# Row sums of two head pairs in one pass of four 32-column tiles, reciprocals spread through DRAM, q and k prep grouped by three pairs

## Chip, cores and metric

One core of a Trainium2 chip. The metric is the device time of one execution in microseconds (us), the median of several runs. A ratio of two kernels is the mean time of the one's fast runs over that of the other's of the same rounds, so it is not quite the ratio of the medians quoted.

## The reference

Cosine attention (8 batches, 12 heads, 448 tokens, head size 64), then a feed-forward layer with exact GELU on the joined heads:

```python
q_n = q / (norm(q) + 1e-6);  k_n = k / (norm(k) + 1e-6)
attn = softmax(q_n @ k_n.T / tau)
x = (attn @ v).transpose(0, 2, 1, 3).reshape(3584, 768)
out = gelu(x @ w_in) @ w_out          # 768 -> 2048 -> 768
```

## The kernel before

Heads go in pairs: six pairs per batch, 48 in all. "Prep" of a pair is: load q and k, square them on GpSimd, reduce on VectorE to squared norms, take roots on ScalarE, scale q and k on two engines at once, transpose on TensorE. Then come scores, exp on ScalarE, row sums with a matrix of ones, values, and the product with the reciprocal sums. After six pairs the batch runs the first product (`hp`). The second product (`op`) of two batches is cut into 224 matmuls that fill gaps in the next two attention stretches.

```python
def square(g):    # all but the first two pairs
    nc.gpsimd.tensor_tensor(sq, t, t, ALU.mult)
...
def scale(g):
    nc.vector.tensor_scalar(se, sr, 1e-6, None, ALU.add)
    nc.vector.reciprocal(rn, se)
    for i, eng in enumerate((nc.gpsimd, nc.vector)):          # q half, k half
        eng.tensor_tensor(qkb[:, i]..., t[:, i], rn[:, i].to_broadcast([CS, 2, NC, D]), ALU.mult)
...
def values(g):
    for dst in (sm, o):                                        # row sums, then values
        for c in range(NC):
            for h in range(2):
                nc.tensor.matmul(dst[h * D:(h + 1) * D, :S],
                                 lhsT=ones if dst is sm else v_t[g][:, h, c, :],
                                 rhs=pt_t[g, c][:, h, :], start=(c == 0), stop=(c == NC - 1))

def normalise(g):
    nc.scalar.activation(ln, sm[:, :S], AF.Ln)
    nc.scalar.activation(rs, ln, AF.Exp, scale=-1.0)
    nc.vector.tensor_tensor(x_t[b][:, p, :], o[:, :S], rs, ALU.mult)
...
for i in range(HP):               # attention(b), one head pair per step (cut)
    scores(g, 0)
    upto("sq", g + 5, square); upto("red", g + 4, reduce)
    ...; values(g - 1); normalise(g - 1)
    scores(g, 2); transposes(g + 1)
    upto("root", g + 3, root); upto("sc", g + 3, scale)
```

## Time and profile before

| | before |
|---|---|
| time, median | 488.59 us (3 runs, 487.79 to 489.39); 488.99 with the later run |
| busy: PE, ACT, DVE, POOL | 97, 66, 41, 40% of the span |
| start of the program to the end of the first hp | 68.84 us |
| end of hp to the next hp, with 128 or 96 op matmuls | 40.09 and 35.78 us |
| an hp stretch | 18.65 us |

The span falls apart into an opening (to the end of the first hp), seven attention stretches (hp end to hp start, called even with 128 op matmuls and odd with 96), seven more hp stretches, and a tail. The prediction shows the lines for the stretches. Three other lines of the opening, which the prediction does not mention, already held the sign of what went wrong. They are a square of GpSimd, and VectorE's and GpSimd's halves of the same scaling (columns: start, length, engine, line, operation):

```profile
42.52 3.75 DVE L139 TENSOR_TENSOR qkb<-qk,rn 112x512 bf16<-112x512 f32 x1
42.20 1.92 POOL L110 TENSOR_TENSOR sq<-qk 112x1024 f32<-112x1024 f32 x1
44.06 1.05 POOL L139 TENSOR_TENSOR qkb<-qk,rn 112x512 bf16<-112x512 f32 x1
```

VectorE's half takes 0.69 us as a rule and took 3.75 here, and GpSimd's took 1.05 where 1.46 is usual. So the two instructions are not independent: in the usual case VectorE goes first and GpSimd's half is 0.4 us longer; here VectorE's came during the square, and GpSimd's half went ahead of it as well.

### The profile page before, as it was taken

The numbers are of one execution on the slowest core, as the hardware profiler recorded it, in microseconds if no ns is written. First come the engines' busy times: TensorE is split into PE (matmuls) and PEld (weight loads), VectorE is DVE, ScalarE is ACT, GpSimd is POOL, SyncE is SP. The second block draws the span as 40 slices with busy tenths as digits, with TensorE's granted clock in tenths as the row PEclk, the third lists the DMA queues.
The fourth block names the chain that finished last, engine by engine and source line by source line (L and its number), as shares of the span: only waits on it lengthen the run. The fifth ranks groups of instructions, "written<-read, shape, count | busy, mean of one in ns | idle before, by whom it ended". The sixth has DMA issues, their size and how long they took to land.

```text
span 487.9 us, 8097 instructions
## 1 busy us (share of the span) xinstructions
PE 474.8 (97%) x3280; PEld 245.2 (50%) x3280; DVE 198.5 (41%) x349; ACT 323.1 (66%) x530; POOL 195.8 (40%) x158
## 2 busy tenths in 40 slices
PE   7599999999999999999999999999999999999996
PEld 4254554455554555455545555455555555445563
DVE  4569116721366115650276213760166502631021
ACT  3498569954887448974688547975688646994400
POOL 5789306840367204860077402780066600610000
PEclk9799999999999999999999999999999999999999
DMA  9699964460165302461054500652045210221022
GB/s 216 141 203 233 234 105 115 108 159 1 28 166 142 80 1 80 117 158 29 0 128 131 156 2 6 171 130 76 0 119 137 52 32 1 53 44 32 1 61 68
DMA packets 42053, 45.35 MB, mean 93 GB/s; under 512 B 3360, under 2 KB 37664, under 8 KB 42016
## 3 DMA queue, kind: packets, MB, share of 16 engines
q1 hardware_dynamic: 27280, 32.81, 22.3%
q0 software_dynamic: 14496, 11.80, 16.1%
q8 instruction: 25, 0.41, 0.4%
q10 hardware_dynamic: 240, 0.23, 0.1%
q14 instruction: 12, 0.10, 0.1%
HBM read 45.61 MB, written 11.01 MB: 116 GB/s over the span
## 4 chain that ended last, share of the span: by engine, by line
PE 88%; DMA 4%; ACT 3%; DVE 2%; POOL 1%; issue 1%; SPq 1%; POOLq 0%
PE op L200 30%; PE hp L299 30%; PE st L161 10%; PE sm L174 7%; PE o L174 6%; PE tp L150 4%; DMA qk<-in_k_dram 4%; ACT pt L164 2%; PE spin L240 1%; DVE x L185 1%; POOL qkb L139 1%; SPq L89 1%; ACT rs L184 1%; DVE qkT L151 1%; ACT ln L182 0%
## 5 line engine op out<-in xcount | busy, mean ns | idle before, releaser
L164 ACT ACTIVATE pt<-st 112x896 bf16<-112x896 f32 x192 | 165.0, 911 | 29.7 <-PE st L161 27.8
L139 POOL TENSOR_TENSOR qkb<-qk,rn 112x512 bf16<-112x512 f32 x48 | 69.4, 1447 | 232.9 <-DVE rn L135 213.4
L200 PE MATMUL op<-wo,g 128*128 128x384 bf16 x896 | 161.3, 326 | 0.0
L299 PE MATMUL hp<-x,wi 128*128 128x448 bf16 x768 | 147.9, 352 | 0.1
L301 ACT ACTIVATE g<-hp 128x448 bf16<-128x448 f32 x128 | 69.6, 544 | 80.2 <-PE hp L299 80.2
L200 PEld LDWEIGHTS <-g 128*128 128x128 bf16 x896 | 81.2, 98 | 62.4 <-issue 15.9
L299 PEld LDWEIGHTS <-wi 128*128 128x128 bf16 x768 | 74.8, 98 | 68.8 <-issue 0.4
L110 POOL TENSOR_TENSOR sq<-qk 112x1024 f32<-112x1024 f32 x46 | 87.7, 1907 | 2.0 <-DMA qk<-in_k_dram 1.4
L151 DVE COPY qkT<-tp 128x896 bf16<-128x896 bf16 x48 | 29.7, 620 | 101.3 <-PE tp L150 101.3
L204 DVE COPY ot<-op 128x384 f32<-128x384 f32 x56 | 31.1, 555 | 92.1 <-PE op L200 92.0
L185 DVE TENSOR_TENSOR x<-o,rs 128x448 bf16<-128x448 f32 x48 | 30.0, 624 | 81.4 <-ACT rs L184 60.1
L161 PE MATMUL st<-qkT 64*112 64x448 bf16 x384 | 60.7, 376 | 1.6 <-DVE qkT L151 0.7
L119 DVE TENSOR_REDUCE nq<-sq 112x16 f32<-112x1024 f32 x47 | 56.9, 1211 | 1.8 <-POOL sq L110 1.8
L174 PE MATMUL sm<-pt,ones 112*64 112x448 bf16 x384 | 45.8, 360 | 0.0
L174 PE MATMUL o<-pt,v 112*64 112x448 bf16 x384 | 44.3, 352 | 0.0
L161 PEld LDWEIGHTS <-qkT 64*112 64x112 bf16 x384 | 20.5, 125 | 39.3 <-issue 28.1
L182 ACT ACTIVATE ln<-sm 128x448 f32<-128x448 f32 x48 | 25.5, 532 | 21.3 <-PE sm L174 21.2
L139 DVE TENSOR_TENSOR qkb<-qk,rn 112x512 bf16<-112x512 f32 x48 | 37.1, 773 | 1.9 <-DMA qk<-in_k_dram 0.2
L97 POOL DMA_DIRECT2D v<-in_v_dram x48 | 34.2, 712 | 0.2 <-issue 0.2
L150 PE MATMUL tp<-ident,qkb 112*128 112x112 bf16 x384 | 27.9, 215 | 5.3 <-DVE qkb L139 4.4
L150 PEld LDWEIGHTS <-qkb 112*128 112x128 bf16 x384 | 20.5, 98 | 20.7 <-issue 13.2
L174 PEld LDWEIGHTS <-ones 112*64 112x64 bf16 x384 | 17.7, 109 | 23.1 <-issue 15.9
(26 smaller groups left out, 162.7 us busy)
## 6 DMA issues: line engine op xcount, KB each, us to landing
qk<-in_q_dram SPq DMA_DIRECT2D x48, 224.0 KB, 2.8
qk<-in_k_dram SPq DMA_DIRECT2D x47, 224.0 KB, 3.8
v<-in_v_dram POOLq DMA_DIRECT2D x48, 112.0 KB, 3.6
wi<-in_moe_w_in_dram POOLq DMA_DIRECT2D x6, 512.0 KB, 10.3
wo<-in_moe_w_out_dram POOLq DMA_DIRECT2D x4, 768.0 KB, 18.9
out_dram<-ot SPq DMA_DIRECT2D x8, 336.0 KB, 3.8
out_dram<-ot SPq DMA_DIRECT2D x8, 288.0 KB, 3.8
out_dram<-ot SPq DMA_DIRECT2D x8, 240.0 KB, 3.2
```

Source lines behind the costliest of these rows:

```text
L110: nc.gpsimd.tensor_tensor(sq, t, t, ALU.mult)
L119: nc.vector.tensor_reduce(nq, sq, mybir.AxisListType.X, ALU.add)
L139: eng.tensor_tensor(qkb[:, i].rearrange("p c h d -> p h c d"), t[:, i], rn[:, i].to_broadcast([CS, 2, NC, D]), ALU.mult)
L150: nc.tensor.transpose(tp[:, i, c, :], qkb[:, i, c].rearrange("p h d -> p (h d)"), ident)
L151: nc.vector.tensor_copy(qkT, tp)
L161: nc.tensor.matmul(st[:, h, :S], lhsT=qkT[rows, 1, c, :], rhs=qkT[rows, 0, :, :], start=True, stop=True)
L164: nc.scalar.activation(pt, st[:, :, :S], AF.Exp, scale=inv_tau)
L174: nc.tensor.matmul(dst[h * D:(h + 1) * D, :S], lhsT=ones if dst is sm else v_t[g][:, h, c, :], rhs=pt_t[g, c][:, h, :], start=(c == 0), st ...
L185: nc.vector.tensor_tensor(x_t[b][:, p, :], o[:, :S], rs, ALU.mult)
L200: nc.tensor.matmul(ps[:, :NH], lhsT=g_t[sb][:, kf, t * 128:(t + 1) * 128], rhs=wo[:, kf, ni * NH:(ni + 1) * NH], start=(kf == 0), stop=(kf ...
L299: nc.tensor.matmul(hp[:, :S], lhsT=wi[:, kd, m * 128:(m + 1) * 128], rhs=x_t[b][:, kd, :], start=(kd == 0), stop=(kd == KD - 1))
L301: nc.scalar.activation(g_t[sb][:, m, hf * S:(hf + 1) * S], hp[:, :S], AF.Gelu)
```

## The change

The intent: four tiles of 32 columns sum the rows of two head pairs in the time of one; reciprocals then exist once per two pairs, so ScalarE does fewer, and a small store to DRAM with two broadcast loads spreads them over the partitions. Prep is grouped so that ScalarE's roots come once per three pairs. Squares and scaling move to other places in the order. The first product puts off the last contraction of four blocks. Cut to its core:

```diff
     def scale(g):
-        (se, rn per pair)
-        for i, eng in enumerate((nc.gpsimd, nc.vector)):
+        for i, eng in enumerate((nc.vector if 0 < g < HP else nc.gpsimd, nc.vector)):
...
+    def sums_two(g):
+        for c in range(NC):
+            for j in range(2):
+                for h in range(2):
+                    r = 32 * (2 * j + h)
+                    nc.tensor.matmul(sm[r:r + 32, :S], lhsT=ones[:, :32], rhs=pt_t[g + j, c][:, h, :],
+                                     start=(c == 0), stop=(c == NC - 1), tile_position=(0, r))
+        rs = reciprocal(g, sm)
+        nc.sync.dma_start(out=rows[g:g + 2]..., in_=rs[0:128:32, :])
+        for h in range(2):
+            nc.sync.dma_start(out=rb[h * D:(h + 1) * D], in_=rows[g:g + 2, h, :].partition_broadcast(D))
...
     (attention, step i of batch b)
-            upto("sq", g + 5, square); upto("red", g + 4, reduce)
+            upto(square, nxt + min(i, 3))          # b > 0; nxt: first pair of the next batch
+            scores(g, 0)
+            upto(scale, min(g + 4, nxt))
+            upto(reduce, nxt + min(max(i - 1, 0), 3))
...
+            if i in (3, 5):
+                for j in (3, 2):
+                    normalise(g - j, nc.vector if b == 0 and i == 5 else nc.gpsimd)
```

More of the change, by code (lines that the diff above doesn't have):

```diff
@@ L46 @@
     wpool = ctx.enter_context(tc.tile_pool(name="wpool", bufs=1))
-    qkp = ctx.enter_context(tc.tile_pool(name="qkp", bufs=6))
+    qkp = ctx.enter_context(tc.tile_pool(name="qkp", bufs=7))
     sqp = ctx.enter_context(tc.tile_pool(name="sqp", bufs=3))
@@ L50 @@
     nrm = ctx.enter_context(tc.tile_pool(name="nrm", bufs=3))
-    qkbp = ctx.enter_context(tc.tile_pool(name="qkbp", bufs=3))
+    qkbp = ctx.enter_context(tc.tile_pool(name="qkbp", bufs=5))
     qkTp = ctx.enter_context(tc.tile_pool(name="qkTp", bufs=3))
-    ptp = ctx.enter_context(tc.tile_pool(name="ptp", bufs=10))
+    ptp = ctx.enter_context(tc.tile_pool(name="ptp", bufs=12))
     rcp = ctx.enter_context(tc.tile_pool(name="rcp", bufs=2))
-    xp = ctx.enter_context(tc.tile_pool(name="xp", bufs=2))
-    gp = ctx.enter_context(tc.tile_pool(name="gp", bufs=2))
+    osp = ctx.enter_context(tc.tile_pool(name="osp", bufs=4))
+    xp = ctx.enter_context(tc.tile_pool(name="xp", bufs=1))
+    gp = ctx.enter_context(tc.tile_pool(name="gp", bufs=1))
     op_ = ctx.enter_context(tc.tile_pool(name="otp", bufs=3))
@@ L60 @@
     ps_mm = ctx.enter_context(tc.tile_pool(name="ps_mm", bufs=2, space=bass.MemoryType.PSUM))
+    rows = nc.dram_tensor("rows", (NG, 2, S), F32, kind="Internal").ap()
     ctx.enter_context(tc.manual_schedule())
@@ L77 @@
     GELU_SET = "gelu_and_others"
-    qk_t, v_t, sq_t, nq_t, sr_t, qkb_t, qkT_t, pt_t, acc_t = {}, {}, {}, {}, {}, {}, {}, {}, {}
+    groups = ([[n] for n in range(HP + 1)] + [list(range(HP + 1, 2 * HP))]
+              + [list(range(n, n + 3)) for n in range(2 * HP, NG, 3)])
+    place = {g: (n, j) for n, gr in enumerate(groups) for j, g in enumerate(gr)}
+    qk_t, v_t, sq_t, nq_t, rn_t, qkb_t, qkT_t, pt_t = {}, {}, {}, {}, {}, {}, {}, {}
+    o_t, os_t, sm_t, rb_t = {}, {}, {}, {}
     x_t, g_t = {}, {}
@@ L113, in reduce @@
         sq = sq_t.pop(g)
-        nq = nrm.tile([CS, 2, 2, NC], F32, tag="nq", name=f"nq{g}")
+        n, j = place[g]
+        if j == 0:
+            nq_t[n] = nrm.tile([CS, len(groups[n]), 2, 2, NC], F32, tag="nq", name=f"nq{n}")
+        nq = nq_t[n][:, j]
         if g == 0:
@@ L119, in reduce, with root @@
             nc.vector.tensor_reduce(nq, sq, mybir.AxisListType.X, ALU.add)
-        nq_t[g] = nq
-    def root(g):
-        nq = nq_t.pop(g)
-        ln = nrm.tile([CS, 2, 2, NC], F32, tag="lq", name=f"lq{g}")
+    def root(n):
+        nq = nq_t.pop(n)
+        shape = [CS, len(groups[n]), 2, 2, NC]
+        ln = nrm.tile(shape, F32, tag="lq", name=f"lq{n}")
         nc.scalar.activation(ln, nq, AF.Ln, bias=tiny)
-        sr = nrm.tile([CS, 2, 2, NC], F32, tag="sr", name=f"sr{g}")
+        sr = nrm.tile(shape, F32, tag="sr", name=f"sr{n}")
         nc.scalar.activation(sr, ln, AF.Exp, scale=0.5)
-        sr_t[g] = sr
-    def scale(g):
-        sr = sr_t.pop(g)
-        se = nrm.tile([CS, 2, 2, NC], F32, tag="se", name=f"se{g}")
-        nc.vector.tensor_scalar(se, sr, 1e-6, None, ALU.add)
-        rn = nrm.tile([CS, 2, 2, NC], F32, tag="rn", name=f"rn{g}")
-        nc.vector.reciprocal(rn, se)
+        se = nrm.tile(shape, F32, tag="se", name=f"se{n}")
+        nc.vector.tensor_scalar(se, sr, 1e-6, None, ALU.add)
+        rn = nrm.tile(shape, F32, tag="rn", name=f"rn{n}")
+        nc.vector.reciprocal(rn, se)
+        rn_t[n] = rn
+    def scale(g):
+        n, j = place[g]
+        rn = rn_t[n][:, j]
         qkb = qkbp.tile([CS, 2, NC, 2, D], BF16, tag="qkb", name=f"qkb{g}")
         t = qk_t.pop(g)
-        for i, eng in enumerate((nc.gpsimd, nc.vector)):
+        for i, eng in enumerate((nc.vector if 0 < g < HP else nc.gpsimd, nc.vector)):
             eng.tensor_tensor(
@@ L157, in scores, with values, reciprocal @@
         for c in (c0, c0 + 1):
-            st = ps_st.tile([CS, 2, 512], F32, tag="st", name=f"st{g}_{c}")
+            st = ps_st.tile([128, 2, 512], F32, tag="st", name=f"st{g}_{c}")
             for h in range(2):
                 rows = slice(h * D, (h + 1) * D)
-                nc.tensor.matmul(st[:, h, :S], lhsT=qkT[rows, 1, c, :], rhs=qkT[rows, 0, :, :],
+                nc.tensor.matmul(st[:CS, h, :S], lhsT=qkT[rows, 1, c, :], rhs=qkT[rows, 0, :, :],
                                  start=True, stop=True)
             pt = ptp.tile([CS, 2, S], BF16, tag="pt", name=f"pt{g}_{c}")
-            nc.scalar.activation(pt, st[:, :, :S], AF.Exp, scale=inv_tau)
+            nc.scalar.activation(pt, st[:CS, :, :S], AF.Exp, scale=inv_tau)
             pt_t[g, c] = pt
-    def values(g):
+    def values(g, copy):
         o = ps_acc.tile([128, 512], F32, tag="o", name=f"o{g}")
-        sm = ps_acc.tile([128, 512], F32, tag="sm", name=f"sm{g}")
-        acc_t[g] = (o, sm)
-        for dst in (sm, o):
-            for c in range(NC):
-                for h in range(2):
-                    nc.tensor.matmul(dst[h * D:(h + 1) * D, :S],
-                                     lhsT=ones if dst is sm else v_t[g][:, h, c, :],
-                                     rhs=pt_t[g, c][:, h, :], start=(c == 0), stop=(c == NC - 1))
-    def normalise(g):
-        b, p = divmod(g, HP)
-        o, sm = acc_t.pop(g)
+        for c in range(NC):
+            for h in range(2):
+                nc.tensor.matmul(o[h * D:(h + 1) * D, :S], lhsT=v_t[g][:, h, c, :],
+                                 rhs=pt_t[g, c][:, h, :], start=(c == 0), stop=(c == NC - 1))
+        os_t[g] = o[:, :S]
+        if copy:
+            os = osp.tile([128, S], F32, tag="os", name=f"os{g}")
+            nc.vector.tensor_copy(os, o[:, :S])
+            os_t[g] = os
+        v_t.pop(g)
+    def reciprocal(g, sm):
         ln = rcp.tile([128, S], F32, tag="ln", name=f"ln{g}")
@@ L184, in normalise, with sums_one @@
         nc.scalar.activation(rs, ln, AF.Exp, scale=-1.0)
-        nc.vector.tensor_tensor(x_t[b][:, p, :], o[:, :S], rs, ALU.mult)
-        v_t.pop(g)
+        return rs
+    def sums_one(g):
+        sm = ps_acc.tile([128, 512], F32, tag="sm", name=f"sm{g}")
         for c in range(NC):
-            pt_t.pop((g, c))
+            for h in range(2):
+                nc.tensor.matmul(sm[h * D:(h + 1) * D, :S], lhsT=ones, rhs=pt_t[g, c][:, h, :],
+                                 start=(c == 0), stop=(c == NC - 1))
+        rb_t[g] = reciprocal(g, sm)
+    def sums_two(g):
+        sm = ps_acc.tile([128, 512], F32, tag="sm", name=f"sm{g}")
+        for c in range(NC):
+            for j in range(2):
+                for h in range(2):
+                    r = 32 * (2 * j + h)
+                    nc.tensor.matmul(sm[r:r + 32, :S], lhsT=ones[:, :32], rhs=pt_t[g + j, c][:, h, :],
+                                     start=(c == 0), stop=(c == NC - 1), tile_position=(0, r))
+        rs = reciprocal(g, sm)
+        nc.sync.dma_start(out=rows[g:g + 2].rearrange("j h s -> (j h) s"), in_=rs[0:128:32, :])
+        rb = osp.tile([128, 2, S], F32, tag="rb", name=f"rb{g}", bufs=2)
+        for h in range(2):
+            nc.sync.dma_start(out=rb[h * D:(h + 1) * D], in_=rows[g:g + 2, h, :].partition_broadcast(D))
+        for j in range(2):
+            rb_t[g + j] = rb[:, j, :]
+            for c in range(NC):
+                pt_t.pop((g + j, c))
+    def normalise(g, eng):
+        b, p = divmod(g, HP)
+        eng.tensor_tensor(x_t[b][:, p, :], os_t.pop(g), rb_t.pop(g), ALU.mult)
     def second_pieces(sb, t):
@@ L227, with upto, roots @@
     weights = [lambda kd=kd: load_wi(kd) for kd in range(KD)] + [lambda i=i: load_wo(i) for i in range(4)]
-    done = {"qk": 0, "v": 0, "sq": 0, "red": 0, "root": 0, "sc": 0}
-    def upto(what, n, f):
-        while done[what] < min(n, NG):
-            f(done[what])
-            done[what] += 1
+    done = {}
+    def upto(f, n, last=NG):
+        while done.get(f, 0) < min(n, last):
+            done[f] = done.get(f, 0) + 1
+            f(done[f] - 1)
+    def roots(n):
+        upto(root, n, len(groups))
     def spin(n):
@@ L246, in run @@
         def run(n):
-            if b == 0:
-                spin(4)
             for _ in range(max(0, min(n, len(fill)))):
@@ L252, in attention @@
         x_t[b] = xp.tile([128, HP, S], BF16, tag="x", name=f"x{b}")
-        tail = 20 if fill else 0
+        tail = 12 if fill else 0
+        nxt = (b + 1) * HP
         for i in range(HP):
@@ L256, in attention @@
             share = (len(fill) - tail) // (HP - i) if i else 30
+            if b == 0:
+                if i > 0:
+                    roots(min(i + 2, HP + 1))
+                upto(square, min(i + 4, HP + 2))
+            else:
+                if i == HP - 1:
+                    roots(2 * b + 7)
+                upto(square, nxt + min(i, 3))
             if g == 0 or i > 0:
                 scores(g, 0)
-            upto("sq", g + 5, square)
-            upto("red", g + 4, reduce)
-            if i > 0:
-                run(share // 3)
-                upto("root", g + 3, root)
-                values(g - 1)
-                normalise(g - 1)
-            else:
-                run(24)
-                upto("root", g + 3 if g else 2, root)
-            if g == 0:
-                upto("sc", 2, scale)
+            if g == 0:
+                roots(2)
+            upto(scale, min(i + 2, HP) if b == 0 else min(g + 4, nxt) if b > 1 or i > 0 else g + 2)
+            upto(reduce, min(i + 3, HP + 2) if b == 0 else nxt + min(max(i - 1, 0), 3))
+            if b == 0:
+                spin(3)
+            if i == 0:
+                run(24)
+            else:
+                run(share // 3)
+                if i == HP - 1:
+                    sums_one(g - 1)
+                values(g - 1, i < HP - 1)
+                if i in (2, 4):
+                    sums_two(g - 2)
+                elif i == HP - 1:
+                    normalise(g - 1, nc.vector)
             scores(g, 2)
+            if b == 0:
+                spin(10 if i == 0 else 2)
             if i < HP - 1:
                 transposes(g + 1)
-            upto("root", g + 3, root)
-            upto("sc", g + 3, scale)
-            upto("qk", g + 9, load_qk)
-            upto("v", g + 4, load_v)
+            upto(load_v, g + 4)
+            if i in (3, 5):
+                for j in (3, 2):
+                    normalise(g - j, nc.vector if b == 0 and i == 5 else nc.gpsimd)
+            upto(load_qk, min(g + 9, nxt + 6))
             for _ in range(2 if b == 0 and i < 4 else 1):
@@ L282, in attention @@
         g = b * HP + HP - 1
-        run(len(fill) - 8)
-        values(g)
-        normalise(g)
         run(len(fill))
+        sums_one(g)
+        values(g, False)
+        normalise(g, nc.vector)
     def first(b):
@@ L293, in first, with mm @@
         nc.scalar.preload_act_table_set(GELU_SET)
+        nxt = (b + 1) * HP
+        hps = {}
+        def mm(m, kds):
+            for kd in kds:
+                nc.tensor.matmul(hps[m], lhsT=wi[:, kd, m * 128:(m + 1) * 128],
+                                 rhs=x_t[b][:, kd, :], start=(kd == 0), stop=(kd == KD - 1))
+        for m in range(2):
+            hps[m] = ps_mm.tile([128, 512], F32, tag="mm", name=f"hp{b}_{m}")[:, :S]
+            mm(m, range(KD - 1))
+        st = ps_st.tile([128, 2, 512], F32, tag="st", name=f"hp{b}_2")
+        for m in range(2, 4):
+            hps[m] = st[:, m - 2, :S]
+            mm(m, range(KD - 1))
+        upto(scale, nxt + 3 if b else nxt + 1)
+        upto(square, nxt + 6)
+        upto(reduce, nxt + 6)
+        for m in range(4):
+            mm(m, (KD - 1,))
         for m in range(KF):
             if m == KF - 5 and b + 1 < B:
-                transposes((b + 1) * HP)
-            hp = ps_mm.tile([128, 512], F32, tag="mm", name=f"hp{b}_{m}")
-            for kd in range(KD):
-                nc.tensor.matmul(hp[:, :S], lhsT=wi[:, kd, m * 128:(m + 1) * 128],
-                                 rhs=x_t[b][:, kd, :], start=(kd == 0), stop=(kd == KD - 1))
-            nc.scalar.activation(g_t[sb][:, m, hf * S:(hf + 1) * S], hp[:, :S], AF.Gelu)
+                transposes(nxt)
+            if m > 3:
+                hps[m] = ps_mm.tile([128, 512], F32, tag="mm", name=f"hp{b}_{m}")[:, :S]
+                mm(m, range(KD))
+            nc.scalar.activation(g_t[sb][:, m, hf * S:(hf + 1) * S], hps.pop(m), AF.Gelu)
+        upto(load_qk, nxt + 7)
         if b + 1 < B:
             nc.scalar.preload_act_table_set(EXP_SET)
-            scores((b + 1) * HP, 0)
-    upto("qk", 1, load_qk)
+            roots(2 * b + 8)
+            scores(nxt, 0)
+    upto(load_qk, 1)
     nc.scalar.preload_act_table_set(EXP_SET)
-    upto("qk", 6, load_qk)
-    upto("v", 3, load_v)
+    upto(load_qk, 4)
     spin(24)
-    upto("sq", 1, square)
-    upto("red", 1, reduce)
-    upto("root", 1, root)
-    upto("sq", 2, square)
-    upto("sc", 1, scale)
+    upto(square, 1)
+    upto(reduce, 1)
+    roots(1)
+    upto(square, 2)
+    upto(scale, 1)
     transposes(0)
-    upto("red", 2, reduce)
-    upto("sq", 4, square)
+    upto(square, 3)
+    upto(load_v, 2)
+    upto(reduce, 2)
+    upto(load_qk, 7)
     fill = []
```

## The prediction

> **What bounds the kernel now.** I read the page's busy shares first, then cut the span into stages at the starts of the first feed-forward product (hp), then read the tensor engine's order of work inside one stage, then the opening stage by itself.
>
> ```profile
> PE 474.8 (97%) x3280; PEld 245.2 (50%) x3280; DVE 198.5 (41%) x349; ACT 323.1 (66%) x530; POOL 195.8 (40%) x158
> ```
>
> PE is the engine to relieve, but 97% busy is not 97% streaming: the same matmul counts as longer while it waits in the pipe. So I take the cost of a block of matmuls from start to start. The batches alternate, because the second product (op) of a pair of batches is spread over the next two attention stretches as 96 and 128 matmuls. An odd stretch and the even one after it, from the end of hp to the next hp (busy us and, in brackets, instructions of PE, PEld, DVE, ACT, POOL):
>
> ```profile
> 295.25:331.12 35.87, 35.77 (x281) 18.05 (x282) 20.83 (x39) 31.54 (x51) 24.13 (x18) 1.00 0.47 119
> 349.69:389.83 40.14, 40.14 (x313) 20.70 (x314) 22.04 (x41) 31.52 (x51) 24.12 (x18) 1.00 0.38 94
> ```
>
> The even one has 32 more op matmuls. At 163 ns (a block of 19 takes 3.19 us start to start, one of 3 takes 0.59) that is 5.2 us, and it is only 4.27 us longer: the odd one loses about 1 us to something else. ACT is busy 31.5 of 35.9 us there, and in its middle it never pauses (rows of the timeline: start, length, engine, line):
>
> ```profile
> 307.92 0.95 PE L174 MATMUL sm<-pt,ones 112*64 112x448 bf16 x8
> 308.70 0.92 PE L174 MATMUL o<-pt,v 112*64 112x448 bf16 x8
> 309.56 0.59 PE L161 MATMUL st<-qkT 64*112 64x448 bf16 x4
> 310.08 0.57 PE L150 MATMUL tp<-ident,qkb 112*128 112x112 bf16 x8
> 310.48 1.14 PE L200 MATMUL op<-wo,g 128*128 128x384 bf16 x6
> 311.55 0.74 PE L161 MATMUL st<-qkT 64*112 64x448 bf16 x4
> 312.22 0.66 PE L200 MATMUL op<-wo,g 128*128 128x384 bf16 x3
> ...
> 308.63 0.31 ACT L125 ACTIVATE lq<-nq,tiny 112x16 f32<-112x16 f32 x1
> 308.97 0.22 ACT L127 ACTIVATE sr<-lq 112x16 f32<-112x16 f32 x1
> 309.10 0.53 ACT L182 ACTIVATE ln<-sm 128x448 f32<-128x448 f32 x1
> 309.65 0.58 ACT L184 ACTIVATE rs<-ln 128x448 f32<-128x448 f32 x1
> 310.14 3.58 ACT L164 ACTIVATE pt<-st 112x896 bf16<-112x896 f32 x4
> ```
>
> Start to start, a row-sum pass (sm) costs PE 0.78 us, values (o) 0.86, a half of the scores (st) 0.52 and transposes (tp) 0.41; the second st, 0.67 instead of 0.52, waits for an exp. ACT's head pair costs 0.47 (roots) + 1.04 (ln, rs) + 3.4 (four exps) = 4.9 us, just the spacing of the pairs. So even stretches are bound by PE, odd ones by ACT for five pairs and by PE for the rest.
>
> The opening is different. hp starts at about 50 us, though the first batch's attention on PE is some 16 us of matmuls. ACT works from 11 us at 5.07 us a head pair, after one hole: it had no scores of pair 1 until 21.1 us. VectorE's order explains it:
>
> ```profile
> 12.31 1.22 DVE L119 TENSOR_REDUCE nq<-sq 112x16 f32<-112x1024 f32 x1 [0.63 <-POOL sq L110]
> 14.66 1.22 DVE L119 TENSOR_REDUCE nq<-sq 112x16 f32<-112x1024 f32 x1 [1.13 <-POOL sq L110]
> 15.80 0.73 DVE L133 TENSOR_SCALAR se<-sr 112x16 f32<-112x16 f32 x1
> 21.14 1.73 ACT L164 ACTIVATE pt<-st 112x896 bf16<-112x896 f32 x2 [5.87 <-PE st L161]
> ```
>
> The roots of pair 1 were ready at 13.2 us, but the reductions of pairs 2 and 3 stand ahead of its scaling, and wait for GpSimd squares that wait for loads.
>
> **What the Trainium skill says.** "TensorE: Matmul & The Clock Gate", Part 3 (Measured speedup vs the span model): three 32-column tiles with 512 streamed columns gave 2.38x, four row tiles 3.07x, not 3 and 4. The trace agrees for two tiles: 8 matmuls of 448 columns in 0.78 us are 195 ns per pair, where hp needs 189 ns for one such matmul. No run here shows four. "TensorEngine Tiling (Array Packing)", Key Properties: changing the tiling mode drains the engine. The trace agrees: 6 op take 1.07 us where 163 ns each make 0.98, so 0.09 us per change of shape, and sm to o, the same shape, pays none. "Advanced Engine Details and Errata", VectorE Performance Modes (Mode Summary): the second VectorE port is shared with GpSimd, and two-port modes and GpSimd block each other. This fits the se above: 0.73 us instead of its usual 0.17, ending with a GpSimd square. [...]The trace's smallest store, 48 KB, lands 3.6 us after issue in the median, so I take 2.2 to 3.5 us for a hop in a quiet stretch.
>
> **The change, part by part.**
>
> *Row sums.* Per batch, six passes become two double passes (16 matmuls of 32 columns for two head pairs) and two single ones. A double pass at four tiles in perfect parallel would be 4 x 0.19 = 0.75, plus one change of shape 0.09: 0.85 us. Its 16 weight loads could bound it instead: eight tp, each with its own load, go at 51 ns apiece, and the loads of sm at about 60, so 16 are 0.8 to 1.0. I choose 0.95. Two pairs cost 1.56 now, so 0.6 us is saved per double pass, 1.2 per batch, all on the path of an even stretch.
>
> *ACT.* Two of six ln/rs pairs go (2 x 1.04) and six root pairs become two (4 x 0.47): 4.0 us of ACT per batch, hidden in even stretches. In odd ones I followed PE and ACT through the new order by hand with the durations above: PE alone needs about 33.5 us, and after each double pass the ln/rs delays the next exps so that one score block waits some 0.35 us. That makes 34.2 against 35.9, 1.7 us saved.
>
> *Start of hp.* The new order runs five of six contractions for four blocks of hp, 20 x 0.189 = 3.8 us, before it needs the last x. Now nothing waits there (x lands at 389.55, its first user starts near 390.8), so this gains nothing. It costs a little: the gelus of those blocks come late, and the fifth block waits for the first one's bank, about 0.2 us a batch.
>
> *The way through DRAM.* From rs: a 7 KB store, two broadcast loads of 224 KB, two multiplications, on GpSimd. Estimate 2.5 + 4 + 2 x 1.0 = 8.5 us. For pairs 2 and 3 of an odd batch, rs ends about 10 us before hp wants x2. It fits, with some 1.5 us to spare, so I count 0. The copies of o to SBUF (0.62 us, DVE) free the bank sooner than the multiplication that waited for rs, and DVE has room.
>
> *The opening.* The scaling of pair 1 now stands before the reduction of pair 2, both halves on DVE (2 x 0.69), so its scores reach ACT at about 17.5 us (16.9 if no square blocks se) instead of 21.1. From there ACT needs 3.4 + 0.47 + 1.04 x 2/3 = 4.6 us a pair, but DVE now has 4.25 (0.17 + 0.25 + 1.38 + 1.21 + 0.62 + 0.62) plus blocking of se by squares, so I take 4.8 instead of 5.07. That brings the last exp to about 41 and hp to 43. But the x of pairs 2 and 3 comes through DRAM with DMA at 93% load, where 224 KB take 7 to 9 us: rs about 35.5, store 38.5, broadcasts 44 to 47, then DVE. x5 stands behind them on DVE. So hp runs freely only from about 46 to 46.5, 4.3 us earlier than now.
>
> *Sum.* Even stretches 3 x 1.2 = 3.6; odd 4 x 1.7 = 6.8; hp starts 7 x -0.2 = -1.4; opening 4.3. Total 13.3 us; I add 0.8 for shorter waits between DVE and PE that I cannot size (the qkT copy no longer queues behind the multiplication). 488.6 - 14.1 = 474.5 us.
>
> **Rivals.** (1) Four tiles do not overlap: the double pass takes 1.5 us or more, PE saves nothing, and only ACT relief in odd stretches (about 1.0 each) and the opening remain: about 481. For it: 16 weight loads, and the skill's 2.38x; against it: loads of sm already run ahead of their matmuls. (2) The DRAM round trip becomes the bound: x2 and x3 late by 2 to 3 us in each odd batch and by more in the first. Then hp waits where it now starts at once, and the gain shrinks by up to 10 us: about 481 to 484. Against it: 10 us of slack, and loads that are far ahead of need in steady batches, so the queue is short. (3) Everything goes better: the double pass takes 0.8, odd stretches lose no exp wait, and the opening ends at 43 because the broadcasts land in 4 us. Then 3 x 1.5 + 4 x 2.7 + 7.5 gives 466.
>
> **Range and chances.** Rival 3 gives the low end and half of rival 1 or 2 the high one: 466 to 481. The 2% line is 478.8. To miss it, a third of the sum must fail; the opening and the odd stretches are separate causes, so I give faster 0.82, same 0.17, slower 0.01.
>
> **What would show it.** In the changed kernel: sums of 32 columns, 16 in 0.85 to 1.0 us start to start (1.5 proves rival 1); even stretches (end of hp to hp) near 38.9 and odd near 34.2; no pause on PE before the third contraction of hp (a pause there, ended by GpSimd, proves rival 2); first scores of pair 1 exponentiated near 17.5; hp running freely from 46. If most of the gain lies in the opening, or if GpSimd's multiplications take far over 1.0 us, my working is wrong even where the total fits.

## The result

The changed kernel takes 532.28 us in the median (4 runs, 529.08 to 533.38) against 488.99 (4 runs): ratio 1.0875, 95% interval 1.0818 to 1.0931. I had predicted 474.5 us and put 1% on slower.

Two rows of the page of the changed kernel (busy share; then the granted clock of TensorE in tenths, in 40 slices):

```profile
PE 479.8 (91%) x3262; PEld 238.9 (45%) x3262; DVE 267.3 (50%) x300; ACT 296.5 (56%) x442; POOL 216.3 (41%) x183
...
PEclk9699699899988999899997999999997999999999
```

VectorE has fewer instructions (300 for 349) and is busy 69 us longer. TensorE's clock drops in nearly every batch; before, it did so only in the first few slices. One group holds most of VectorE's surplus, first before and then after (count, then busy us and mean ns):

```profile
L139 DVE TENSOR_TENSOR qkb<-qk,rn 112x512 bf16<-112x512 f32 x48 | 37.1, 773 | 1.9 <-DMA qk<-in_k_dram 0.2
```

```profile
L150 DVE TENSOR_TENSOR qkb<-qk,rn 112x512 bf16<-112x512 f32 x53 | 103.9, 1988 | 0.4
```

The shape is the same, the mean 2.6 times as long. Inside an even stretch of the changed kernel, VectorE and GpSimd at the same time:

```profile
147.94 7.09 DVE L150 TENSOR_TENSOR qkb<-qk,rn 112x512 bf16<-112x512 f32 x1
155.95 0.61 DVE L162 COPY qkT<-tp 128x896 bf16<-128x896 bf16 x1
...
147.32 1.91 POOL L117 TENSOR_TENSOR sq<-qk 112x1024 f32<-112x1024 f32 x1
149.18 1.04 POOL L150 TENSOR_TENSOR qkb<-qk,rn 112x512 bf16<-112x512 f32 x1
150.16 0.71 POOL L104 DMA_DIRECT2D v<-in_v_dram  x1
150.90 1.91 POOL L117 TENSOR_TENSOR sq<-qk 112x1024 f32<-112x1024 f32 x1
152.75 1.04 POOL L150 TENSOR_TENSOR qkb<-qk,rn 112x512 bf16<-112x512 f32 x1
153.74 0.70 POOL L104 DMA_DIRECT2D v<-in_v_dram  x1
154.45 2.32 POOL L117 TENSOR_TENSOR sq<-qk 112x1024 f32<-112x1024 f32 x1
```

VectorE's scaling lasts from 147.94 to 155.03, while GpSimd works through squares, scalings and loads with no pause. It takes 0.69 us when nothing holds it, so by that estimate it was let in at 154.34, near the end of GpSimd's sixth instruction in these lines, and the square behind that one took 2.32 us where the two before took 1.91. The copy of the transposed q and k stands behind it on VectorE and comes at 155.95. TensorE waits for that copy:

```profile
156.61 0.99 PE L172 MATMUL st<-qkT 64*112 64x448 bf16 x4 [2.96 <-DVE qkT L162]
157.54 1.78 PE L241 MATMUL op<-wo,g 128*128 128x384 bf16 x5
159.25 1.71 PE L182 MATMUL o<-pt,v 112*64 112x448 bf16 x8
160.89 1.68 PE L215 MATMUL sm<-pt,ones 112*32 112x448 bf16 x16
...
173.25 0.94 PE L215 MATMUL sm<-pt,ones 112*32 112x448 bf16 x16
```

After 2.96 us without work every block takes nearly twice as long: the row sums 1.68 us, and 0.94 later in the same stretch. The view by stretches gives the granted clock for it (after the brackets; the columns are start:end, length, busy us of PE, PEld, DVE, ACT, POOL):

```profile
141.75:186.66 44.91, 41.70 (x314) 20.25 (x313) 23.31 (x28) 27.15 (x38) 20.49 (x19) 0.92 0.41 94
...
156.61:162.50 5.89, 5.89 (x33) 1.84 (x33) 2.94 (x4) 1.73 (x2) 0.83 (x2) 0.50 0.70 167
```

For 5.89 us the clock was 0.50. So a wait costs twice: once as a wait, and once as slow matmuls after it.

The spans of the two traces differ by 41.9 us. By parts, all from starts and ends of hp: the opening +10.2 (79.07 for 68.84); the first odd stretch +8.0 (43.80 for 35.77); the next two odd ones +4.4 each; the three even ones +4.8 each; the last odd one -1.2; seven hp stretches +0.23 each. The last attention stretch is a control that the kernel brings along: there is no next batch, so GpSimd has no squares, and there the change gains.

### The profile page after: what moved, and what is told of

It is laid out like the page before. It is cut to its first block, busy times and chain, and to the rows that moved or that the text cites. A ratio compares the mean times of both kernels' runs of the same rounds, so it can differ in the third digit from the quotient of the medians.

```text
span 529.8 us, 7998 instructions
## 1 busy us (share of the span) xinstructions
PE 479.8 (91%) x3262; PEld 238.9 (45%) x3262; DVE 267.3 (50%) x300; ACT 296.5 (56%) x442; POOL 216.3 (41%) x183
## 4 chain that ended last, share of the span: by engine, by line
PE 77%; DVE 13%; ACT 4%; issue 3%; DMA 3%; POOL 0%; SPq 0%; DVEq 0%
PE hp L359 27%; PE op L241 25%; DVE qkb L150 8%; PE st L172 7%; PE o L182 7%; PE tp L161 4%; PE sm L215 3%; PE sm L203 2%; ACT ln L193 2%; DVE qkT L162 2%; DMA rb<-rows 1%; ACT g L381 1%; DVE os L187 1%; PE spin L284 1%; DMA qk<-in_q_dram 1%
## 5 line engine op out<-in xcount | busy, mean ns | idle before, releaser
L241 PE MATMUL op<-wo,g 128*128 128x384 bf16 x896 | 164.5, 332 | 0.0
L359 PE MATMUL hp<-x,wi 128*128 128x448 bf16 x768 | 152.3, 357 | 7.1 <-DVE x L229 6.6
L150 DVE TENSOR_TENSOR qkb<-qk,rn 112x512 bf16<-112x512 f32 x53 | 103.9, 1988 | 0.4
L117 POOL TENSOR_TENSOR sq<-qk 112x1024 f32<-112x1024 f32 x46 | 95.5, 2088 | 3.7 <-DVE nq L129 2.8
L229 POOL TENSOR_TENSOR x<-os,rb 128x448 bf16<-128x448 f32 x30 | 33.4, 1128 | 154.2 <-DMA rb<-rows 119.1
L150 POOL TENSOR_TENSOR qkb<-qk,rn 112x512 bf16<-112x512 f32 x43 | 49.9, 1171 | 109.7 <-PE op L241 83.0
L182 PE MATMUL o<-pt,v 112*64 112x448 bf16 x384 | 49.7, 384 | 1.1 <-DVE x L229 1.1
L172 PEld LDWEIGHTS <-qkT 64*112 64x112 bf16 x384 | 20.4, 129 | 61.7 <-issue 32.0
L193 ACT ACTIVATE ln<-sm 128x448 f32<-128x448 f32 x32 | 17.4, 544 | 48.4 <-PE sm L215 25.6
L139 DVE TENSOR_SCALAR se<-sr 112x48 f32<-112x48 f32 (+2 forms) x20 | 8.0, 402 | 62.2 <-ACT sr L137 61.9
L187 DVE COPY os<-o 128x448 f32<-128x448 f32 x32 | 19.8, 620 | 24.1 <-PE o L182 24.1
## 6 DMA issues: line engine op xcount, KB each, us to landing
wi<-in_moe_w_in_dram POOLq DMA_DIRECT2D x6, 512.0 KB, 10.9
```

What stands on the lines that cost most here:

```text
L150: eng.tensor_tensor(qkb[:, i].rearrange("p c h d -> p h c d"), t[:, i], rn[:, i].to_broadcast([CS, 2, NC, D]), ALU.mult)
L172: nc.tensor.matmul(st[:CS, h, :S], lhsT=qkT[rows, 1, c, :], rhs=qkT[rows, 0, :, :], start=True, stop=True)
L182: nc.tensor.matmul(o[h * D:(h + 1) * D, :S], lhsT=v_t[g][:, h, c, :], rhs=pt_t[g, c][:, h, :], start=(c == 0), stop=(c == NC - 1))
L241: nc.tensor.matmul(ps[:, :NH], lhsT=g_t[sb][:, kf, t * 128:(t + 1) * 128], rhs=wo[:, kf, ni * NH:(ni + 1) * NH], start=(kf == 0), stop=(kf ...
L359: nc.tensor.matmul(hps[m], lhsT=wi[:, kd, m * 128:(m + 1) * 128], rhs=x_t[b][:, kd, :], start=(kd == 0), stop=(kd == KD - 1))
```

## The experiments

Theory A: from batch 1 on, VectorE's half of the scaling, which reads two tensors from SBUF, is shut out while GpSimd works (the lock-out, below). What stands behind it comes late, TensorE waits, and then runs at the lower clock. Theory B, the second rival of the prediction: the round trip through DRAM does the harm.

| run | edit | time | ratio to before | first hp ends | even | odd |
|---|---|---|---|---|---|---|
| before | | 488.99 | | 68.84 | 40.09 | 35.78 |
| changed kernel | | 532.28 | 1.0875 | 79.07 | 44.91 | 40.18 |
| scale_pool | all scaling on GpSimd, b > 0 | 495.54 | 1.014 | 80.04 | 39.17 | 34.47 |
| prep_only | sums as before | 516.85 | 1.057 | 66.97 | 42.4 to 44.0 | 38.3, 41.3 |
| filler | dummy matmuls in the wait | 522.32 | 1.067 | 80.22 | 42.20 | 38.62 |
| sums_only | prep as before | 494.81 | 1.012 | 77.84 | 39.17 | 35.21 |
| control_one_input | one SBUF input for two (wrong result) | 493.03 | 1.008 | 76.35 | 39.16 | 34.46 |
| first_x_pool | scale_pool, first x on GpSimd | 492.87 | 1.008 | 76.76 | 39.17 | 34.46 |
| one_square_buffer | squares: 1 buffer for 3 | 495.07 | 1.013 | 77.08 | 39.16 | 34.47 |
| scale_vector | all scaling on VectorE | 495.73 | 1.014 | 78.91 | 39.16 | 34.46 |
| scale_first | scaling ahead of the square | 506.35 | 1.036 | 80.02 | 39.16 | 35.81 |
| combined | scale_pool, no DRAM in batch 0 | 483.01 | 0.988 | 66.51 | 39.16 | 34.46 |
| combined_plain_hp | combined, hp as before | 481.90 | 0.986 | 67.47 | 39.18 | 34.47 |

Even and odd are the stretches of batches 2, 4, 6 and of 3 and 5; where one number stands they agree within 0.02 us. At the limit of 2%, the changed kernel, prep_only, filler and scale_first count as slower and all others as the same; the intervals of the two combined kernels lie wholly below 1.

### scale_pool: from batch 1 on, VectorE reads no two SBUF tensors in one instruction

```diff
-        for i, eng in enumerate((nc.vector if 0 < g < HP else nc.gpsimd, nc.vector)):
+        for i, eng in enumerate((nc.vector if 0 < g < HP else nc.gpsimd, nc.vector if g < HP else nc.gpsimd)):
```

> The changed kernel with one edit: from batch 1 on, both halves of the q and k scaling run on GpSimd, so VectorE has no instruction there that reads two tensors from SBUF. Theory A (VectorE's scaling is shut out while GpSimd works through a queue of squares and scalings, 7.1 us instead of 0.7, and everything behind it on VectorE is late): the 3 to 6.5 us waits of PE for the scores of a batch's third pair go, and with them the slow clock after them; batches 1 to 6 lose 5 to 9 us each less, so the time falls from 532 to about 493 (485 to 500). What stays is the late start of the first batch's hp. Theory B (the round trip through DRAM holds up x or the queues): no change, 528 or more.

495.54 us, 36.7 less than the changed kernel. Even and odd stretches fall to 39.17 and 34.47 us, the clock stays up, and GpSimd carries both halves in the time it has:

```profile
134.62:173.79 39.17, 38.91 (x314) 19.68 (x313) 15.29 (x25) 27.14 (x38) 22.81 (x22) 1.00 0.47 108
```

Theory B is ruled out as the main cause: the round trip is still there. What stays is the opening, 80.04 us.

### prep_only: the sums and the round trip taken out

```diff
-                values(g - 1, i < HP - 1)
-                if i in (2, 4): sums_two(g - 2)
-                elif ...
+                sums_one(g - 1); values(g - 1, False); normalise(g - 1, nc.vector)
-            if i in (3, 5): (normalise from the broadcast rows)
```

> The changed kernel with the row sums, ln/rs and normalising of before (one pass per pair, nothing through DRAM), the new prep kept. Theory A: the scaling is still shut out, the waits for the third pair stay, and batches 1 to 6 stay at 58 to 65 us; only the first batch's hp starts earlier, by some 5 us or more, and the sums cost 1 us a batch more: 525 to 540. Theory B: the round trip is gone, so the time falls to 490 or less.

516.85 us, 8 us below the range of theory A, because the opening is 12 us shorter (66.97 us, even shorter than before) and some stretches lose less. But the stalls remain without any DRAM traffic of ours: five scalings on VectorE of 7.09 us, one of 9.36. So the new prep alone (its grouping and its order together) carries the harm of the steady batches, and the new sums with their round trip that of the opening.

### filler: how much of it is the clock

```diff
             st = ps_st.tile([128, 2, 512], F32, ...)
+            for _ in range(14 if HP <= g < NG - HP and g % HP == 2 and c == 0 else 0):
+                nc.tensor.matmul(st[:CS, 0, :S], lhsT=ident, rhs=blank, start=True, stop=True)
```

> The changed kernel with 14 dummy matmuls (2.7 us at full clock) ahead of the first score matmuls of the third pair in batches 1 to 6, where PE sits idle for 3 to 6.5 us. They overwrite a score bank that the real matmuls then start anew; the result stays right. Theory A2 (about half of what each wait costs is the lower clock of PE for the microseconds after it): the matmuls after the wait run at their usual length (op 0.99 us for 5 instead of 1.78, values 0.95 instead of 1.71), and the time falls by 8 to 14 us to about 521. Against it (the lower clock lies beside the wait and costs nothing): same time or slower by what the dummies exceed the wait.

522.32 us, 10.0 less, by doing more work. The sums behind the wait take their usual time (the same place as above):

```profile
155.86 2.81 PE L171 MATMUL st<-blank,ident 112*112 112x448 bf16 x14
159.00 0.59 PE L174 MATMUL st<-qkT 64*112 64x448 bf16 x4 [0.32 <-DVE qkT L162]
159.51 0.99 PE L243 MATMUL op<-wo,g 128*128 128x384 bf16 x5
160.43 0.95 PE L184 MATMUL o<-pt,v 112*64 112x448 bf16 x8
161.31 0.94 PE L217 MATMUL sm<-pt,ones 112*32 112x448 bf16 x16
```

Of the 5.74 us that an even stretch loses (44.91 - 39.17), 2.71 are the clock (44.91 - 42.20) and 3.03 the wait; of 5.71 in an odd one, 1.56 and 4.15. The granted clock of the changed kernel agrees: it is 0.50 for 6.8 us around the end of each wait of 2.96 us, but for only 3.4 us after each wait of 4.1 us in the odd stretches, and in the filler's trace it is 1.00 from batch 2 to 6.

### sums_only: the row sums without the new prep

The kernel before with `sums_two`, the copies of o and the normalising on GpSimd, and its own prep.

> The kernel before with the new row sums alone (double passes, copies of o, round trip through DRAM, normalising on GpSimd), the prep and its order as before. Theory A: the scaling halves are spread out as before and collide little, so the steady batches gain the 1 to 1.5 us each of the double passes unless GpSimd, waiting for the broadcast rows, delays a scaling; the first batch loses up to 5 us to the round trip: 478 to 490. Theory B: the round trip does the harm, 510 or more.

494.81 us, some 5 us above the range. The steady part gains 0.92 and 0.57 us a stretch (39.17 and 35.21), where 1 to 1.5 a batch was expected, and no scaling on VectorE takes over 0.7 us. The miss lies in the opening, 9.0 us longer than before. The 7 KB store of the reciprocals of pairs 2 and 3 was issued at 42.36 us, the broadcasts that wait for it at 49.74, and their rows reached VectorE at 57.95:

```profile
42.36 0.55 SPq L211 DMA_DIRECT2D rows<-rs  x1
49.74 1.24 SPq L214 DMA_DIRECT2D rb<-rows  x2
```

```profile
57.95 1.61 DVE L222 TENSOR_TENSOR x<-os,rb 128x448 bf16<-128x448 f32 x2 [2.33 <-DMA rb<-rows]
```

15.6 us from the store's issue to use, while the opening's loads keep the DMA engines busy for 0.95 of the time (42 to 58 us). So theory B is right for the first batch only.

### control_one_input: is it the second input?

```diff
+            if i == 1 and g >= HP:      # wrong result on purpose: k is not scaled (cut)
+                nc.vector.tensor_reduce(qkb[:, i]..., t[:, i].rearrange("p h c (d o) -> p h c d o", o=1), X, ALU.add)
+                continue
```

> Control for theory A, with a wrong result on purpose: in the changed kernel, from batch 1 on, VectorE's half of the scaling (two SBUF inputs, k and 1/norm) is replaced by a reduction over an axis of one element: the same place in the order, the same 112x512 read and written, but a single SBUF input. GpSimd's queue is as in the changed kernel. Theory A (the instruction is shut out because it reads two tensors from SBUF while GpSimd works): the replacement takes 0.6 to 0.9 us wherever it stands, attention stretches of batches 2 to 6 fall from 44.9 and 40.2 to 39.2 and 34.5 us as with all scaling on GpSimd, total 493 to 498. Rival C (VectorE's order or a late semaphore holds it, whatever it reads): the 3 to 4 us waits stay, 525 or more.

493.03 us, stretches 39.16 and 34.46. The one-input instruction takes 667 ns in the mean of 42, in the same place and beside the same GpSimd queue:

```profile
L152 DVE TENSOR_REDUCE qkb<-qk 112x512 bf16<-112x512 f32 x42 | 26.9, 667 | 0.0
```

Order and semaphores of VectorE are thus not the cause. The control also changes the kind of instruction, and two things speak to that. In the kernel before, the 48 multiplications of o, which lies in PSUM, by the reciprocals in SBUF are of the same kind as the scaling but have one SBUF input: they took 606 to 627 ns in every run with them, also where they began in the middle of a square or a scaling of GpSimd (21 times in the trace before). And in the control's own trace a multiplication of two SBUF tensors in the opening still took 5.17 us, where a free one takes 0.62. So it is that the instruction reads two tensors from SBUF. This kernel's result is wrong and its k larger, so its time is taken for the waits alone.

### first_x_pool and combined: the opening

```diff
 first_x_pool (on top of scale_pool)
-                    normalise(g - j, nc.vector if b == 0 and i == 5 else nc.gpsimd)
+                    normalise(g - j, nc.gpsimd)
 combined (on top of scale_pool)
-                if i == HP - 1: sums_one(g - 1)
-                values(g - 1, i < HP - 1)
+                if b == 0 or i == HP - 1: sums_one(g - 1)
+                values(g - 1, b > 0 and i < HP - 1)
                 (sums_two only for b > 0; otherwise normalise(g - 1, nc.vector))
```

> The kernel with all scaling of batches 1 to 7 on GpSimd, and one edit more: the normalising of pairs 2 and 3 of the first batch on GpSimd, ahead of its squares, instead of on VectorE, where the two instructions took 6.1 us beside the squares. Theory A: x of these pairs is ready some 2 us after the broadcast rows land (52.6 us), not 6; the first hp stretch ends 3 to 4 us earlier (76 to 77 instead of 80), 492 in total. Rival (the late landing of the rows alone sets this): no change, 495.

> All scaling of batches 1 to 7 on GpSimd, and no round trip through DRAM in the first batch: it sums pair by pair as before and normalises on VectorE; later batches keep the double passes. If the losses are separate and add up: the first hp stretch ends at about 67 us as in the run with the old sums, the steady batches take 58.05 and 53.35, 482.5 in total (480 to 485), faster than before by 1.2%. If the first batch is bound by something else in this order: 488 or more.

first_x_pool: 492.87 us, the first hp ends at 76.76 instead of 80.04, as expected. This was the second place of the same lock-out: in the changed kernel the two multiplications by the broadcast rows took 5.6 us on VectorE, beside three squares on GpSimd:

```profile
52.42 5.58 DVE L229 TENSOR_TENSOR x<-os,rb 128x448 bf16<-128x448 f32 x2 [2.97 <-DMA rb<-rows]
```

combined: 483.01 us, ratio 0.9882 (0.9864 to 0.9899), 0.5 us above the expectation. The losses of the opening and of the steady batches are separate and add up.

### combined_plain_hp: the put-off contraction

The combined kernel with the plain loop over blocks of hp and eight op matmuls after the last values, both as before.

> The combined kernel with the first product in the plain order of before (no block put off its last contraction) and 8 matmuls of the second product after the last values. hp stretches take 18.6 instead of 18.9 us, so 8 x 0.2 to 0.3 us less than the combined kernel: about 480.5. If the put-off contraction hides a wait for the last x that the plain order shows: the same or up to 2 us slower.

481.90 us, ratio 0.9859 (0.9836 to 0.9881). An hp stretch takes 18.65 instead of 18.89 us in batches 2 to 6, as expected; in batch 1 it takes 19.10. This is the fastest version. Its interval overlaps that of combined, so the last microsecond rests on the stretches rather than on the totals.

### one_square_buffer, scale_vector, scale_first: when is VectorE let in?

```diff
 one_square_buffer
-    sqp = ctx.enter_context(tc.tile_pool(name="sqp", bufs=3))
+    sqp = ctx.enter_context(tc.tile_pool(name="sqp", bufs=1))
 scale_vector
-        for i, eng in enumerate((nc.vector if 0 < g < HP else nc.gpsimd, nc.vector)):
+        for i, eng in enumerate((nc.vector if g > 0 else nc.gpsimd, nc.vector)):
 scale_first (b > 0)
+            upto(scale, ...)
             upto(square, nxt + min(i, 3))
             scores(g, 0)
-            upto(scale, ...)
```

> The changed kernel with one buffer for the squares instead of three, nothing else: GpSimd's next square must wait until VectorE has reduced the one before, so its queue can no longer run on for 7 to 12 us. Theory A in its sharper form (VectorE's two-input instruction gets in at the first pause of GpSimd's queue, so its delay is the length of GpSimd's run without a pause): the longest scaling on VectorE in batches 2 to 6 falls from 7.1 us to 4 or less, and the attention stretches from 44.9 and 40.2 to 40 to 42 and 35 to 38 us, although a buffer was taken away; the first batch may lose some us. If pauses do not matter: stretches as before or longer.

> The changed kernel with both halves of the scaling on VectorE in all batches but for the first pair; GpSimd keeps squares, loads of v and normalising. If the trouble were that the two halves are split over two engines, this would mend it as the run with all scaling on GpSimd does (stretches of 39.2 and 34.5 us). Theory A says that the squares alone shut VectorE out, and that twice as many of its instructions are exposed: stretches of 42 to 46 and 38 to 41 us, 515 to 540 in total.

> The changed kernel with one swap: from batch 1 on, the scaling of a step is issued ahead of its square instead of behind it. Both engines keep their halves, and GpSimd has the same instructions and three square buffers. In the runs so far VectorE's two-input instruction was let in at the next boundary of GpSimd's queue (delay up to 2.4 us in all) when it came during a square followed by a square or a load, or during a scaling half; it was held over several instructions (2.8 to 9.4 us) only when it came during a square with a scaling half next. Theory A in this form: the swap takes that sequence away, no scaling on VectorE takes over 3 us in batches 2 to 6, stretches fall to 39.2 and 34.5 us, 494 to 500 in total. If GpSimd simply holds VectorE off for as long as its queue has no pause: scalings of 5 us or more stay, stretches 43 and 38 or more, 515 or more.

one_square_buffer: with two buffers less, GpSimd has to pause, the longest scaling in batches 2 to 6 falls from 7.09 to 2.85 us, and the stretches fall to 39.16 and 34.47, better than I expected. The kernel became 37 us faster by losing buffers.

scale_vector: a miss. I had said that squares alone shut VectorE out. They delay it by at most one square: no scaling in batches 2 to 6 took more than 2.38 us (0.69 plus the rest of a square of 1.9), and TensorE did not wait. VectorE did all the scaling here, so a lack of room on VectorE is not the cause either. In these batches the harm appeared only with squares and GpSimd's own scaling halves in one queue. That is no general condition: in the openings of the changed kernel and of scale_pool, a multiplication of two SBUF tensors took 3.35 and 3.91 us beside squares alone, past the end of one square and the whole of the next.

scale_first: a miss of both forms. From the earlier traces I had drawn the rule that only a square followed by a scaling half keeps VectorE out over several instructions. With that sequence gone, each of batches 2 to 6 still had one scaling of 3.30 us and, later, one of 4.43 (it came during a square with a load next, and was let in only as another square ended). Neither 494 to 500 nor 515 came, but 506.35. Those holds cost the even stretches nothing (39.16 us) and the odd ones 1.34; most of the loss is in the attention stretch of batch 1, 45.5 us against 35.7 in scale_pool, where two scalings took 5.57 and 5.96. So the cause is settled, and the rule by which VectorE is let in between two instructions of GpSimd is not.

## Why the prediction was wrong

**Row sums: right.** The double pass takes 0.87 us start to start (29.01 to 29.88), where I chose 0.95. The even stretch gains 0.92 (40.09 to 39.17 with the lock-out gone), where I had 1.2: after a double pass the transposes start 0.71 us after the scores instead of 0.52. In the chain of waits they stand behind ScalarE's ln, which reads the sums from the bank that the transposes use:

```profile
162.63 0.55 ACT ln L193
...
163.22 0.55 PE tp L161 x8
```

**ScalarE: right, with the lock-out gone.** Odd stretches of 34.47 us against the predicted 34.2, so 1.31 us gained (35.78 - 34.47) where I had 1.7. The first odd stretch gains nothing in scale_pool (35.70), though it does in control_one_input (34.46); why stays open.

**Start of hp: right.** +0.23 us a batch against +0.2.

**The step that failed: "DVE has room".** I added up VectorE's busy time and kept its scaling at 0.69 us wherever it stood. I knew from the trace that a two-port instruction (se) waits for GpSimd, and cited it, but took the two-input instructions for free of that. The change itself made the collisions: before, GpSimd's half waits for the same reciprocal as VectorE's, and VectorE goes first; the grouped reciprocals free both halves of three pairs at a time, GpSimd runs ahead without a pause, and VectorE arrives in the middle. So the traces read; no run parts the grouping from the new order. That is 5.74 us in each of three even stretches, 5.71 in each of two odd ones and 8.1 in the first (43.80 - 35.70): 36.7 us. Within it I also had no term for the clock, 2.7 us of each even stretch.

**The opening: wrong.** I had hp running freely from 46 us; it did so from 58.06. The scores of pair 1 reached ScalarE at 20.4 us, not 17.5: pair 1's se took 2.14 us beside a square, its first scaling 2.05, and the next root waited 4.7 us for the reduction behind them. The scores of the next three pairs came 17.6 us later (19.70 to 37.27), not 14.4. So the store of the reciprocals of pairs 2 and 3 was issued at 41.54 us, not about 35.5. The way through DRAM then took 10.9 us, within the 8.5 to 11.5 that I had allowed, and the rows landed at 52.4. (In batches 1 to 7 the broadcasts could be issued 1.7 to 2.9 us after the store, against the 2.2 to 3.5 that I took for a hop; here it was 2.8.) The two multiplications took 5.58 us, where two free ones take 1.25. Last, hp itself ran 63 matmuls in 15.01 us, which at 0.189 us each would be 11.9: the clock again.

**The rivals.** None named the lock-out. The second named the round trip, with the right place and a fair size, but only the opening has it: in batches 1 to 7 of scale_pool hp starts without a pause. My range had a slip: half of either rival gives 478 to 480, and its upper end of 481 is the whole of the first. The sum of what was right, 13 us of gain hoped for, is 7 us in the best version. The opening's 4.3 shrank to 1.4 (67.47 for 68.84).

**Still open:** why VectorE is let in at the next boundary of GpSimd's queue in some sequences and only after up to eight instructions in others. Nor is it shown which instructions of GpSimd count: in the changed kernel's opening a scaling took 2.05 us from 15.34 us on, while GpSimd only issued loads (14.91 to 17.40).

## What to carry to other kernels

Before regrouping work on two engines that share data paths, list which instructions of the one read two tensors from SBUF, and what the other may be doing at that time once its waits are gone: waits that look idle can be what keeps two engines apart. An instruction with an odd duration, here one of 3.75 us among 0.69, is a measurement of such a bond and is worth an explanation before the change. And a wait of TensorE can cost more than its length: waits of 2.96 us cost 5.74 us here, and those of 4.1 us cost 5.71.

## What the Trainium skill lacked or had wrong

- "Advanced Engine Details and Errata", GPSIMD Details, does say that GpSimd conflicts with VectorE instructions in a two-port mode "or with two SBUF inputs". My prediction used only the note on modes. That passage gives no size, but "SBUF — State Buffer", Summary: rules for kernel authors, does: where VectorE has two SBUF inputs and the GpSimd instruction reads SBUF, the second to issue is blocked until the first finishes. That is too short here: in many cases the wait did end with one instruction (a scaling of 0.69 us then took up to 2.4), but scalings took 7.09 and 9.36 us beside runs of six and eight instructions; a one-input instruction in the same place took 0.67.
- "TensorE: Matmul & The Clock Gate", Part 1, puts the fall of the clock at an idle window of about 3.4 us, and its closing table at gaps of about 3. Here a wait of 2.96 us, in each of three even stretches, was enough for 5.9 us at 0.50. Its Part 3 has no figure for four column tiles: 16 matmuls of 448 columns took 0.87 us, 3.5 times as fast as 16 at hp's 0.189 us each.
- No page that I found says how long a small store through DRAM takes behind weight loads: 7 KB stored and 448 KB spread took 10.9 us to arrive in one trace and 15.6 in another, against 3.8 us in the median for a broadcast load alone. Of the 15.6, 7.4 went by before the broadcasts could be issued, against a median of 1.7 in batches 1 to 7.
